# VectorE in place of GpSimd for the low parts of the second MoE's first weights

## The chip, the cores and the metric

The kernel runs on one core of one Trainium2 chip. The metric is the time of one execution in microseconds (us) on the device, the median of several runs. A core has five engines that run side by side, each through its own list of instructions: TensorE (PE; its weight loads are shown as PEld), VectorE (DVE), ScalarE (ACT), GpSimd (POOL) and SyncE (SP), which here issues DMA transfers. An engine takes its instructions strictly in the order in which the program issued them; a wait holds everything behind it on that engine.

## The reference

Three stages in float32, one behind the other:

```python
attn = attention(q_l, k_l, v_l, q_g, k_g, v_g)       # 2 x 544 tokens, 8 heads of 64
x = (attn @ w_a * (attn @ w_b)) @ w_out              # "first MoE": 1088 x 512, d_ff 1536
logits = x @ w_gate                                  # router, 8 experts
expert = argmax(logits); gate = softmax(logits)[expert]
h = relu(x_of_expert @ w1[expert])                   # 512 x 1024 per expert, capacity 288
out = gate * (h @ w2[expert])                        # "second MoE"
```

A token keeps its place in its expert by counting the tokens ahead of it; those over the capacity give zeros. TensorE multiplies in a reduced format (float32r), so each float32 matrix is split in a high part (the value rounded to float32r) and a low part (the rest), and each product is made of three passes: high by high, high by low, low by high.

## The kernel before, in words

`moe1` ends with `down`, the second half of the product with `w_out` (the call with `last`). It goes over nine token tiles: tile 0 (64 tokens, 12 matmuls) and tiles 1 to 8 (128 tokens, 18 matmuls of 128x512 each: six blocks of d_ff by three passes). When a tile's matmuls are through, VectorE adds the result to what the first half left (L797). Behind each matmul `c` (1 to 18) of tile `i` (1 to 8), `steps(i, c, fs)` issues whatever else is due there. `c` is called the step below. All is issued in a fixed order (a manual schedule), so the place of a call in `steps` sets its place in each engine's queue.

Most of it is the router of the tiles before, in three parts whose places are in `ROUTE_AT`:

- `route_t(j)`: four transposes of tile j's rows on TensorE (L905), and the split of the result. For tiles 0 to 4 that is three bf16 parts: ScalarE L887, VectorE L888, ScalarE L889, and later, at step 3 of the tile after, VectorE's `rest` (L892). Tiles 5 to 8 have one copy on ScalarE (L907).
- `route_l(j, k)`: the logits on TensorE (L925 for tiles 0 to 4, L920 for the rest), then some seven small VectorE instructions (L938 to L955) that make the one-hot of the best expert (`roh`, L943) and the count so far (`cnt`, L950, two buffers).
- `route_s(j)`: small matmuls that count places (L963, L966), which need the one-hot and the count, then VectorE makes the slot number (L972, L982, L985; for tiles 6 to 8 also `to`, L978), and GpSimd scatters the tile's rows into their slots in DRAM by an indirect DMA (L988). Tile 5's `route_s` also queues on SP a load of the first 128 slots (`x2c`, L992), which waits for the scatters so far.

In tiles 2 to 5 the logits of tile i-2 and the transposes of tile i-1 come at step 8 (tile 2: steps 6 and 12) and the slots of tile i-2 at step 17 (tile 2: step 12). In tile 6 step 6 has the transposes of tile 5, step 8 the logits of tile 4, step 12 those of tile 5, step 17 the slots of tile 4. In tile 7: step 6 the slots of tile 5 and the transposes of tile 6, step 12 the logits of tile 6. In tile 8: step 6 the transposes of tile 7, step 12 the slots of tile 6 and the logits of tile 7. What is left comes behind the last matmul.

`steps` also prepares the first weights of the second MoE. These come in units of 512x512 (`wt[q]`, four per expert: two of w1, two of w2), each in two halves of 128x1024. For a half, `moe2_first(q, hf)` has ScalarE copy the raw weights to the high part (L566) and GpSimd subtract it from them for the low part (L567). Behind a unit's second half SP is given the load of unit q+4 into the same raw buffer (L572), which therefore waits for L567. The halves of units 0 to 3 are made two per tile at step 2 of tiles 1 to 4, those of unit 4 at steps 9 and 12 of tile 8. The order of work behind that, `moe2`, has semaphores of its own and isn't touched: there VectorE makes most low parts (L1633) and GpSimd one unit per expert (L1778). Its block begins when SP has seen everything ahead of it done.

Of the kernel before, what the change touches and what calls it, by code (L numbers as in the profile page):

```python
# [12 lines left out]
ALU = mybir.AluOpType  # L13
# [11 lines left out]
ROUTE_AT = ((12, 24, 30), (12, 26, 35), (8, 26, 35), (8, 26, 35), (8, 26, 35), (6, 12, 24), (6, 12, 30), (6, 12, 20))  # L25
REST_AT = 21

CONV2_AT, CONV2, CONV2_LAST = 2, (2, 2, 2, 2, 0, 0, 0, 0), (9, 12)

FIRST, FILL = (3, None, 2), (3, 2, 5, 2)  # L30
WARM = (0, 0, 0, 1, 2)
# [7 lines left out]
def attn_moe_moe_kernel(  # L39
# [18 lines left out]
    nc = tc.nc  # L58
# [11 lines left out]
    NTT = (NT + P - 1) // P  # L70
# [466 lines left out]
    NU = 2 * NH  # L537
# [8 lines left out]
    def raw_at(q):  # L546

        return q % NR0 if q < NIN - NXR or not NXR else (q - NIN) % NRAW
# [8 lines left out]
    wt = []  # L557
    raw = []
# [1 line left out]
    xs = []  # L560
    ptx = []

    def moe2_first(q, hf):
        r = raw[raw_at(q)]
        hs = slice(2 * hf, 2 * hf + 2)
        nc.scalar.copy(out=wt[q][:, 0, hs], in_=r[:, hs])  # L566
        nc.gpsimd.tensor_tensor(out=wt[q][:, 1, hs], in0=r[:, hs], in1=wt[q][:, 0, hs], op=ALU.subtract)  # L567
        if hf == 1 and q < NU:
            moe2_load(q + NR0)

    def moe2_load(q, ks=slice(0, 4)):
        nc.sync.dma_start(out=raw[raw_at(q)][:, ks], in_=unit_src(q)[:, ks])  # L572
# [133 lines left out]
    def moe1():  # L706
        with ExitStack() as mx:
# [37 lines left out]
            def steps(i, c, fs):  # L745

                for j in range(max(0, i - 3), min(i, NTT - 1)):
                    at = c + 3 * len(fs) * (i - 1 - j)
                    t, l, r = ROUTE_AT[j]
                    if at == t:  # L750
                        route_t(j)
                    if at == l:
                        for k in range(KD):
                            route_l(j, k)
                    if at == REST_AT and j < N_BF16:
                        rest.pop(j)()
                    if at == r:
                        route_s(j)
                if c == CONV2_AT:
                    o = sum(CONV2[:i - 1])  # L760
                    for k in range(o, o + CONV2[i - 1]):
                        moe2_first(k // 2, k % 2)
                if i == NTT - 1 and c in CONV2_LAST:
                    moe2_first(NU, CONV2_LAST.index(c))

            def down(fs, first, last):
                for x, i in enumerate([*range(1, NTT), 0] if first else range(NTT)):
# [6 lines left out]
                    for f in fs:  # L774
                        if i == 0:
                            parts = ((t[0:2 * n], gtl[f], 0), (t[0:n], gtl[f][:, 0:n], 1))
                        else:
                            parts = tuple((t, g_t[f][:, gi, o:o + n], wi) for gi, wi in passes)
                        for ot, l, wi in parts:
                            nc.tensor.matmul(  # L780
                                out=ot, lhsT=l, rhs=wo[f][:, wi],
                                start=(c == 0), stop=(c == nm - 1), skip_group_check=True)
                            c += 1
                            if last and i > 0:
                                steps(i, c, fs)
# [18 lines left out]
                if last:  # L804
# [22 lines left out]
                    for at in range(3 * len(fs) + 1, 100):  # L827
                        steps(NTT - 1, at, fs)
# [17 lines left out]
                out=x2[:, :, DM + 1:DM + 2], in_=tokid.rearrange("p (t o) -> p t o", o=1))  # L846
# [49 lines left out]
            def route_t(i):  # L896
                n = tok(i)[1]
                x3 = m2.tile([P, KD, 3, P], BF16, tag="rx", name="rx")
                xs = as_f32(x3)
                nh = 2 if i == NTT - 1 else 1  # L900
                for h in range(nh):
                    tx = ps.tile([P, KD // nh, P], F32, tag="rt", name="tx")
                    for j in range(KD // nh):
                        k = h * KD // nh + j
                        nc.tensor.transpose(tx[:, j, 0:n], row(i)[0:n, k * P:(k + 1) * P], ident[0:n, 0:n])  # L905
                    if i >= N_BF16:
                        nc.scalar.copy(out=xs[:, h * KD // nh:(h + 1) * KD // nh, 0:n], in_=tx[:, :, 0:n])  # L907
                if i >= N_BF16:
                    xss[i] = xs
                else:  # L910
                    rest[i] = split3(tx[:, :, 0:n], tx[:, :, 0:n], x3[:, :, :, 0:n])
                    xss[i] = x3
# [85 lines left out]
            for s in range(NGA * HC, len(slots1)):  # L998
                f, c = slots1[s]
                k = s - NGA * HC  # L1000
# [11 lines left out]
                if s == len(slots1) - 1:  # L1012
# [8 lines left out]
                    for q in range(NR0):  # L1021
# [6 lines left out]
                        out=late_x["x"][:, :, DM + 1:DM + 2],  # L1028
                        in_=tokid[:, NTT - 2:NTT].rearrange("p (t o) -> p t o", o=1))
# [821 lines left out]
```

## Time and profile before

| | before |
|---|---|
| median of 3 runs | 499.58 us (498.74 to 504.02) |
| the profiled execution | 499.53 us, span 497.8 us |
| mean granted TensorE clock | 0.976 |
| TensorE busy | 465.2 us (93% of the span) |
| VectorE, ScalarE, GpSimd busy | 299.2, 262.1, 238.4 us |

The span goes from the first to the last instruction in the trace; the time of the execution has some 2 us around it. Busy times of TensorE are modelled, since matmuls are pipelined. The granted clock is a share of 2.4 GHz; 0.5 is the lower of its two levels, 1.2 GHz, and a value between is a mean over a stretch. In a row of the trace the arrow between names goes from inputs to output (`wt<-raw`), `xN` counts instructions that are merged in the row, and what stands in brackets at the end is the idle time of the engine ahead of it and what ended it.

### The profile page before, as it was taken

What the parts mean: (1) busy time and instruction counts of PE and PEld (TensorE: products, weight loads), DVE (VectorE), ACT (ScalarE), POOL (GpSimd) and SP (SyncE); (2) the same over time, 40 slices, a digit from 0 to 9 for tenths busy, and PEclk for the clock granted to TensorE, in tenths of its full rate; (3) what the DMA queues carried; (4) which work ended last, traced back from release to release, by engine and by line L of the source; (5) the groups of instructions that cost most, each with busy time, mean ns of one, the idle gap of its engine ahead of it and who ended that gap; (6) DMA issues with size and microseconds to landing.
All of it is one profiled execution on the core that took longest, in us unless ns stands there. A gap on an engine that the chain in (4) does not pass through costs nothing.

```text
span 497.8 us, 8982 instructions
## 1 busy us (share of the span) xinstructions
PE 465.2 (93%) x3137; PEld 393.6 (79%) x3137; DVE 299.2 (60%) x668; ACT 262.1 (53%) x580; POOL 238.4 (48%) x247
## 2 busy tenths in 40 slices
PE   8899999999999999999999977987979979999993
PEld 6676778899999988899999855776657757768783
DVE  5758799751676456766663269654666537668420
ACT  3878887653444333533333433223677648677330
POOL 2334547542467514555555576146277437366203
PEclk9999999999999999999999989898989989999997
DMA  7794544130688624553504253332698499493001
GB/s 175 177 224 120 144 121 117 50 129 1 205 233 230 191 86 126 165 175 127 170 1 156 98 181 115 118 124 82 163 374 324 134 297 362 134 392 122 9 6 68
DMA packets 76464, 77.53 MB, mean 156 GB/s; under 512 B 39426, under 2 KB 51714, under 8 KB 76392
## 3 DMA queue, kind: packets, MB, share of 16 engines
q1 hardware_dynamic: 74424, 72.32, 47.3%
q0 software_dynamic: 1968, 4.29, 2.3%
q8 instruction: 40, 0.66, 0.6%
q14 instruction: 32, 0.26, 0.2%
HBM read 63.77 MB, written 14.25 MB: 157 GB/s over the span
## 4 chain that ended last, share of the span: by engine, by line
PE 87%; DVE 6%; issue 3%; ACT 1%; DMA 1%; POOL 0%; SPq 0%; POOLq 0%
PE ab L680 29%; PE o L780 13%; PE ph L1385 13%; PE py L1385 11%; PE px L418 4%; PE s L357 3%; PE tp L402 3%; PE pth L1370 2%; DVE rv L940 2%; PE sgm L338 1%; PE og L478 1%; PE ptx L1353 1%; PE tk L263 1%; PE tq L279 1%; DMA kr<-in_k_l_dram 1%
## 5 line engine op out<-in xcount | busy, mean ns | idle before, releaser
L680 PE MATMUL ab<-xT,wab 128*128 128x272 f32 x1152 | 148.6, 290 | 0.0
L680 PEld LDWEIGHTS ab<-xT,wab 128*128 128x128 f32 x1152 | 145.4, 188 | 3.0 <-issue 2.3
L1385 PE MATMUL py<-wt,ht 128*128 128x512 f32 x224 | 57.3, 402 | 0.0
L392 POOL TENSOR_TENSOR pn<-sm,rs 128x384 f32<-128x384 f32 (+1 forms) x32 | 28.6, 895 | 55.8 <-DVE rs L391 36.0
L688 ACT COPY a_sb<-ab 128x272 f32<-128x272 f32 x48 | 18.6, 387 | 68.3 <-PE ab L680 68.3
L695 DVE TENSOR_TENSOR gf<-a_sb,ab 128x272 f32<-128x272 f32 x48 | 20.8, 433 | 51.8 <-PE ab L680 29.7
L780 PE MATMUL o<-wo,g_all 128*128 128x512 f32 x192 | 51.6, 412 | 0.0
L641 POOL TENSOR_TENSOR wab<-cvs,wab 128x512 fp32r<-128x512 f32 x24 | 34.7, 1446 | 27.7 <-ACT wab L640 27.7
L1385 PEld LDWEIGHTS py<-wt,ht 128*128 128x128 f32 x224 | 39.4, 180 | 10.8 <-issue 0.2
L641 POOL TENSOR_TENSOR g_all<-gf,g_all 128x272 fp32r<-128x272 f32 x32 | 27.7, 866 | 39.5 <-ACT g_all L640 39.5
L1633 DVE TENSOR_TENSOR wt<-raw,wt 128x1024 fp32r<-128x1024 f32 x34 | 42.2, 1297 | 4.1 <-ACT wt L1495 4.0
L780 PEld LDWEIGHTS o<-wo,g_all 128*128 128x128 f32 x192 | 37.0, 196 | 8.3
L631 DVE TENSOR_SCALAR cvs<-cvs 128x512 int32<-128x512 int32 x36 | 32.4, 901 | 16.1 <-ACT cvs L626 16.1
L1226 POOL DMA_INDIRECT out_dram<-x2l,ids x14 | 22.6, 1616 | 40.5 <-DVE dummy L1656 22.7
L1495 ACT CAST wt<-raw 128x1024 fp32r<-128x1024 f32 x40 | 39.3, 1055 | 0.1
L634 DVE SCALAR_TENSOR_TENSOR cvs<-raw,cvs 128x512 int32<-128x512 int32 x36 | 38.3, 1063 | 1.2
L1385 PE MATMUL ph<-wt,xs 128*128 128x512 f32 (+1 forms) x128 | 37.4, 411 | 0.5 <-issue 0.5
L380 ACT ACTIVATE sm<-sm,mn 128x192 f32<-128x192 f32 (+1 forms) x64 | 29.4, 462 | 0.2
L357 PE MATMUL s<-kz,qz 128*128 128x192 f32 (+1 forms) x128 | 29.2, 349 | 0.1
L1385 PEld LDWEIGHTS ph<-wt,xs 128*128 128x128 f32 (+1 forms) x128 | 22.9, 183 | 7.7 <-issue 1.3
L632 DVE SCALAR_TENSOR_TENSOR cvs<-raw,cvs 128x512 int32<-128x512 int32 x36 | 26.8, 744 | 1.2
L370 DVE CUSTOM_DVE_ANT_0 sm<-s,mask 128x192 f32<-128x192 f32 (+1 forms) x64 | 21.5, 372 | 9.4 <-PE s L357 8.4
(219 smaller groups left out, 830.8 us busy)
## 6 DMA issues: line engine op xcount, KB each, us to landing
raw<-in_moe_w_dram SPq DMA_DIRECT2D x31, 1024.0 KB, 7.7
slots_dram<-zrow SPq DMA_DIRECT2D x24, 257.0 KB, 6.1
raw<-in_moe_w_a_dram SPq DMA_DIRECT2D x12, 512.0 KB, 4.0
raw<-in_moe_w_b_dram SPq DMA_DIRECT2D x12, 512.0 KB, 3.9
raw<-in_moe_w_out_dram SPq DMA_DIRECT2D x12, 512.0 KB, 4.0
xr<-slots_dram SPq DMA_DIRECT2D x11, 256.0 KB, 2.7
kr<-in_k_l_dram SPq DMA_DIRECT2D x16, 128.0 KB, 2.9
qr<-in_q_l_dram SPq DMA_DIRECT2D x16, 128.0 KB, 2.9
```

Of the source, the lines that this page charges most:

```text
L357: nc.tensor.matmul(out=s[:, h, 0:width(t)], lhsT=qz[i % 2][:, h, t * P:(t + 1) * P], rhs=kz[i % 2][:, t, 0:width(t)], start=True, stop=True)
L380: nc.scalar.activation(out=sm[:, h, 0:w], in_=sm[:, h, 0:w], func=ACTF.Exp, scale=-1.0, bias=mn[:, h:h + 1], accum_out=su[:, h:h + 1])
L392: nc.gpsimd.tensor_tensor(out=pz[:, :, 0:w], in0=sm[:, :, 0:w], in1=rs.rearrange("p (h o) -> p h o", o=1).to_broadcast([P, 2, w]), op=ALU. ...
L631: nc.vector.tensor_scalar(out=s, in0=s, scalar1=3, scalar2=None, op0=ALU.logical_shift_left)
L632: nc.vector.scalar_tensor_tensor(out=s, in0=l, scalar=29, in1=s, op0=ALU.logical_shift_right, op1=ALU.bitwise_or)
L634: nc.vector.scalar_tensor_tensor(out=s, in0=h, scalar=-0x80000000, in1=s, op0=ALU.bitwise_and, op1=ALU.bitwise_or)
L641: nc.gpsimd.tensor_tensor(out=lo, in0=src, in1=hi, op=ALU.subtract)
L680: nc.tensor.matmul(out=t, lhsT=wab[f][:, j, wi, k * P:(k + 1) * P], rhs=xT[:, xi, k, cs], start=(n == 0), stop=(n == 3 * KD - 1))
L780: nc.tensor.matmul(out=ot, lhsT=l, rhs=wo[f][:, wi], start=(c == 0), stop=(c == nm - 1), skip_group_check=True)
L1385: m = tensor.matmul(out=o, lhsT=l, rhs=w(k, wi)[:, cols], start=(k == 0 and i == 0), stop=(k == nk - 1 and i == len(parts) - 1), skip_grou ...
L1495: scalar.copy(out=wt[q % NSLOT][:, 0, 2 * hf:2 * hf + 2], in_=raw[raw_at(q)][:, 2 * hf:2 * hf + 2]).then_inc(sem["sa"], 1)
L1633: m = vector.tensor_tensor(out=wt[q % NSLOT][:, 1, hk], in0=raw[raw_at(q)][:, hk], in1=wt[q % NSLOT][:, 0, hk], op=ALU.subtract)
```

## The change

`moe2_first` is cut in two: `moe2_hi` (ScalarE, as before) and `moe2_lo`, the same subtraction on VectorE, with the load behind the second half as before. The places change too. High parts of units 0 to 3: one half at step 12 of each of tiles 1 to 4, two at step 12 of tiles 5 and 6. The low part of a half comes in the tile after its high part, at step 4, where there are two also at step 14. Unit 4: high parts at steps 6 and 7 of tile 8, low parts at steps 9 and 11. Within a step the router's calls are issued first.

```diff
-CONV2_AT, CONV2, CONV2_LAST = 2, (2, 2, 2, 2, 0, 0, 0, 0), (9, 12)
+SPLIT2, LO_AT, HI_AT = (0, 1, 1, 1, 1, 2, 2, 0), (4, 14), 12
+HI_LAST, LO_LAST = (6, 7), (9, 11)
...
-    def moe2_first(q, hf):
-        r = raw[raw_at(q)]
+    def moe2_hi(q, hf):
         hs = slice(2 * hf, 2 * hf + 2)
-        nc.scalar.copy(out=wt[q][:, 0, hs], in_=r[:, hs])
-        nc.gpsimd.tensor_tensor(out=wt[q][:, 1, hs], in0=r[:, hs], in1=wt[q][:, 0, hs], op=ALU.subtract)
+        nc.scalar.copy(out=wt[q][:, 0, hs], in_=raw[raw_at(q)][:, hs])
+
+    def moe2_lo(q, hf):
+        hs = slice(2 * hf, 2 * hf + 2)
+        nc.vector.tensor_tensor(
+            out=wt[q][:, 1, hs], in0=raw[raw_at(q)][:, hs], in1=wt[q][:, 0, hs], op=ALU.subtract)
         if hf == 1 and q < NU:
             moe2_load(q + NR0)
...
-                if c == CONV2_AT:
-                    o = sum(CONV2[:i - 1])
-                    for k in range(o, o + CONV2[i - 1]):
-                        moe2_first(k // 2, k % 2)
-                if i == NTT - 1 and c in CONV2_LAST:
-                    moe2_first(NU, CONV2_LAST.index(c))
+                if c == HI_AT and i < NTT - 1:
+                    o = sum(SPLIT2[:i])
+                    for k in range(o, o + SPLIT2[i]):
+                        moe2_hi(k // 2, k % 2)
+                if i == NTT - 1 and c in HI_LAST:
+                    moe2_hi(NU, HI_LAST.index(c))
+                if i == NTT - 1 and c in LO_LAST:
+                    moe2_lo(NU, LO_LAST.index(c))
+                if c in LO_AT[:SPLIT2[i - 1]]:
+                    k = sum(SPLIT2[:i - 1]) + LO_AT.index(c)
+                    moe2_lo(k // 2, k % 2)
```

## Rows read from the trace of the kernel before

**Rows 1.** Stretches: us; busy PE, PEld, DVE, ACT, POOL; clock; DMA share; GB/s.

```profile
290.00:300.00 10.00, 7.73 (x42) 6.15 (x42) 6.70 (x16) 3.94 (x7) 7.22 (x4) 0.83 0.54 197
300.00:310.00 10.00, 6.31 (x43) 4.61 (x42) 9.14 (x22) 3.34 (x6) 6.51 (x4) 1.00 0.41 131
310.00:315.00 5.00, 5.00 (x30) 3.76 (x30) 3.32 (x14) 1.23 (x4) 0.99 (x1) 0.66 0.75 262
```

**Rows 2.** The chain that ended last: start us, us, what.

```profile
304.88 4.44 DVE rv L940
...
336.75 2.38 DVE to L978
```

**Rows 3.** Timeline of VectorE, tiles 5 and 6: start, us, engine, line, what.

```profile
313.88 0.18 DVE L938 TENSOR_REDUCE rlo<-lg 128x8 f32<-128x24 f32 x1 [1.45 <-PE lg L925]
...
315.25 0.70 DVE L888 TENSOR_TENSOR tx<-tx,rx 128x512 f32<-128x512 f32 x1
...
316.61 0.17 DVE L972 CUSTOM_DVE_ANT_0 rv<-lg,roh 128x8 f32<-128x8 f32 x1 [0.66 <-PE lg L966]
...
317.79 0.68 DVE L892 TENSOR_TENSOR rx<-tx,rx 128x512 bf16<-128x512 f32 x1
...
319.97 0.23 DVE L940 SCALAR_TENSOR_TENSOR rv<-rlo,rs,desc 128x8 f32<-128x8 f32 x1
...
322.67 0.16 DVE L950 TENSOR_TENSOR cnt<-cnt,roh 128x8 bf16<-128x8 bf16 x1 [0.40 <-PE lg L966]
```

**Rows 4.** Timeline of GpSimd and VectorE, tiles 4 and 8.

```profile
304.58 4.69 POOL L567 TENSOR_TENSOR wt<-raw,wt 128x1024 fp32r<-128x1024 f32 x2
...
332.05 2.38 POOL L567 TENSOR_TENSOR g_all<-raw,g_all 128x1024 fp32r<-128x1024 f32 x1 [2.66 <-ACT g_all L566]
332.20 2.31 DVE L978 TENSOR_SCALAR to<-cols,rs 128x128 f32<-128x128 f32 x1
```

**Rows 5.** TensorE's waits, 284 to 342 us: total us, times, longest.

```profile
PE lg L963 <- DVE roh L943: 5.0, 3, 2.8
PE lg L963 <- DVE cnt L947: 3.1, 1, 3.1
```

**Rows 6.** Low parts by line: count, duration ns min/median/max, first and last start.

```profile
L567 POOL TENSOR_TENSOR wt<-raw,wt x8: 2339/2390/2643, 282.6 to 306.9; 128x1024 fp32r<-128x1024 f32 x8
...
L1633 DVE TENSOR_TENSOR wt<-raw,wt x34: 1206/1219/3426, 353.9 to 460.5; 128x1024 fp32r<-128x1024 f32 x34
```

**Rows 7.** The chain again, tile 5 from its start.

```profile
310.01 3.49 PE o L780 x9
313.50 0.34 PE lg L925 x12
313.84 0.59 PE tx L905 x4
314.44 2.09 PE o L780 x9
```

**Rows 8.** Timeline of TensorE, tile 7 step 6 and behind tile 8.

```profile
324.19 0.10 PEld L963 LDWEIGHTS <-utri 128*128 128x128 bf16 x1 [0.27 <-DVE x L797]
...
335.74 0.18 PE L963 MATMUL lg<-roh,utri 128*128 128x8 bf16 x1 [1.53 <-DVE roh L943]
```

**Rows 9.** Scatters: timeline in the second MoE, and L988 by line.

```profile
421.08 4.63 DVE L1633 TENSOR_TENSOR wt<-raw,wt 128x1024 fp32r<-128x1024 f32 x4
...
421.42 1.76 POOL L1226 DMA_INDIRECT out_dram<-x2l,ids  x1 [1.09 <-DVE ht L1682]
...
L988 POOL DMA_INDIRECT slots_dram<-x,rsi x7: 974/992/1111, 294.0 to 335.2; - x7
```

**Rows 10.** SP: timeline, longest waits; stretch of the last loads.

```profile
332.14 0.94 SPq L572 DMA_DIRECT2D raw<-in_moe_w_dram  x2
...
SPq L1283 <- DVE cnts L880: 2.6, 1, 2.6
...
334.00:336.00 2.00, 0.47 (x5) 0.27 (x5) 1.82 (x11) 0.69 (x3) 1.21 (x2) 1.00 1.02 357
```

## Prediction

> **What bounds the kernel now.** I read the stretches first, then the chain of waits, then what ran beside each long piece of that chain. The last down-projection, with the router of the second MoE threaded through it, runs from about 278 to 342 us. TensorE is the pace-setter there, but two parts of it go badly [rows 1]: between 290 and 310 us TensorE is busy 7.73 + 6.31 of 20 us, and in 290 to 300 and 310 to 315 its granted clock averages 0.83 and 0.66, where 300 to 310 has 1.00.
>
> The chain says what TensorE waits for [rows 2]: VectorE's instructions on a 128x8 or 128x128 tile, which should be tiny: 4.44 us of L940 and 2.38 of L978 are the longest. The same line L940 takes 0.23 us in a quiet tile [rows 3]. The neighbours tell why [rows 4]: GpSimd's pair of low-part subtractions (L567) runs from 304.58 to 309.27, and the L940 that began at 304.88 ends at 309.32; the next one runs from 332.05 to 334.43, and the L978 that began at 332.20 ends at 334.51. So it isn't GpSimd's 2.39 us as such [rows 6] that costs: certain VectorE instructions of the router stand still until GpSimd's instruction is over, and TensorE stands behind them. The list of TensorE's waits gives the bill [rows 5]: 3.1 us for the first count and 5.0 us in three waits for the one-hot (2.8 the longest; 1.53 of them is the one in tile 8 [rows 8]).
>
> **What the change takes away.** All ten L567 leave GpSimd (10 x 2.39 us); its only work left in these tiles is the scatters. The long L940, L943 and L978 should fall to about 0.23 to 0.35 us. Waits gone: 3.1 + (5.0 - 1.53) = 6.6 us; I leave the 1.53 us of tile 8 aside, since low parts stand there after the change too.
>
> The low clock goes with the long waits: the low stretches follow waits of 3.1 and 2.8 us, while those of 0.7 (5.0 - 2.8 - 1.5) and 1.5 us are followed by full clock. The lost clock is 10 x 0.17 + 5 x 0.34 = 3.4 us, which at 1.2 instead of 2.4 GHz is 6.8 us of time at the low level. Nine matmuls and what stands between them took 3.49 us at the low level and 2.09 at the high one [rows 7], so 40% of these 6.8 us is lost: 2.7 us. Gain so far: 9.3 us.
>
> **What the change adds.** VectorE gets ten subtractions of 128x1024. The same operation in the second MoE takes 1.22 us, the median of 34 [rows 6]: 12.2 us of VectorE in all. ScalarE's ten high-part copies only move (to step 12 of tiles 1 to 6 and steps 6 and 7 of tile 8), and nothing on TensorE's path stands behind them in ScalarE's queue until the next tile's step 6 or 8, so they cost nothing while that tile's VectorE is on time.
>
> *Tiles 2 to 5, one low part each at step 4.* It stands in VectorE's queue behind the addition of the tile before and the router's third part (L892), and ahead of the router's logits (L938). A tile's VectorE work in a quiet tile [rows 3]: L972 to L985 and the addition 1.18 (316.61 to 317.79), L892 0.68, L938 to L888 1.37 (313.88 to 315.25), L888 0.70: 3.93 us, with the low part 5.15. TensorE's tile [rows 7]: 18 matmuls at 2.09/9 = 0.23 make 4.18, logits 0.34, transposes 0.59: 5.11. As good as even: VectorE falls back 0.04 us a tile, and the one-hot, ready some 4 us into the tile, is asked for only behind the 17th matmul, at 4.9. I take 0.1 us for tile 2, where it is asked for at step 12, and nothing for tiles 3 to 5. From both sides: nothing, and 1.22 us each, 4.9 us, if it stood wholly in the way.
>
> *Tile 6, two.* The second, at step 14, stands behind L950, which waits for TensorE at step 17 (0.40 us of waiting in the trace of before [rows 3]); so it begins at the end of the tile, and the five small instructions of tile 4's slots and the addition of tile 6 come 1.22 us later. TensorE waits for that addition already (0.27 us, at 324.19 [rows 8]), in front of step 6's transposes in tile 7. So all of it is exposed: 1.2 us. At least 0 (if the low part found room earlier), at most 1.22.
>
> *Tile 7, two.* The second stands ahead of tile 7's addition again, but there the logits come earlier in the tile, and the addition ends some 1.9 us into tile 8 where its transposes want it at about 1.4: 0.45 us. Between 0 and 1.22.
>
> *Tile 8, two.* The first high part can't come before ScalarE has copied step 6's transposes, as before, when GpSimd began the low part at 332.05 [rows 4]. Two on VectorE last from there to 334.5, just when GpSimd let L978 go before. Behind them L972 and L978 (0.2 + 0.35 us) are still to come, so the one-hot of tile 7 is 0.6 us later and TensorE's wait about 2.1 instead of 1.53 us. Then the second L978 isn't held for 2.38 us any more [rows 2], which brings 0.3 us back, limited by the logits it ran beside. Net 0.35. Between a gain of 1.5 and a loss of 1.3 us.
>
> *Transfers.* Weights of units 4 to 7 are now loaded when VectorE has made the low part. The last (tile 7, step 14) stands on SP's queue behind the load of the first rows from the slots, which waits for tile 5's scatter; so it goes out with the two halves that left at 332.14 [rows 10], and one more MB lands in front of them. At the 357 GB/s of 334 to 336 us that is 2.9 us. SP's last wait at the entry of the second MoE was 2.6 us for the counts [rows 10], so the transfers had landed by then; with the tail 0.35 later the cover is 2.95. I take nothing; without the cover it costs its 2.9 us. Units 5 and 6 have more than a tile to spare.
>
> *Scatters.* GpSimd writes the scatters' descriptors while VectorE subtracts: in the second MoE such a scatter takes 1.76 us where these take 0.99, while the four subtractions beside it stay at 4.63 / 4 = 1.16 [rows 9]. So a scatter may lose 0.8 us, on an engine with nothing else to do, and VectorE nothing. The Trainium skill, SBUF — State Buffer, section Who interferes with whom, says that a VectorE instruction with two SBUF inputs contends with a GpSimd instruction that reads SBUF, and that the second to issue stands fully still; by that a low part, which has two SBUF inputs, could be held by a scatter. The rows here show the scatter slowed, not the low part; no run here shows the opposite.
>
> Sum: 9.3 - 0.1 - 1.2 - 0.45 - 0.35 = 7.2 us. The profiled execution took 499.53 us (span 497.8), beside a median of 499.58: 499.53 - 7.2 = 492.3.
>
> **The rivals.**
> 1. *VectorE's queue becomes the bound in every tile.* 5.15 against 5.11 us says it could; for it: VectorE is busy 9.14 of 10 us in 300 to 310 already [rows 1], against it: most of that is the hold itself. If tiles 2 to 5 and 7 lose 0.7 us each beyond the above, 3.5 us: 495.8.
> 2. *Slower: each low part delays the router's chain whole.* Place: VectorE's queue, at each of the ten. Price: 12.2 us, and the waits stay long enough that the clock still falls, so only 6.6 is gained: 499.5 - 6.6 + 12.2 = 505.1. It decides from an excess of 0.66 us per low part on. Against it: the low part stands at step 4, and the one-hot is wanted at step 17.
> 3. *The holds aren't GpSimd's doing* and stay: nothing gained, 2.1 lost: 501.6. Against it: the two ends agree to 0.1 us.
> 4. *The late loads hold the entry*: up to 2.9 us: 495.2; likelier 1 us, 493.3. For it: the cover is as large as the transfer.
> 5. *Scatters hold the low parts*: seven by 0.99, 6.9 us: 499.2. Against it [rows 9]. The page named above would have it so.
>
> **How the numbers follow.** The forecast 0.67 (490 to 494.4), rival 4 0.08, rival 1 0.12, rival 2 0.06, rival 3 0.04, rival 5 0.03. About 1% (5 us) is what a measurement here can tell from no change. The forecast and rival 4 lie below 494.6: faster 0.75. Rivals 1, 3 and 5 lie within 1%: 0.19. Rival 2 lies above: 0.06. The range: at the low end the whole 9.3 plus the 1.5 us of tile 8, 488.7, rounded to 489; at the high end rival 1, with some room, 496.5; what lies outside is rivals 2, 3 and 5, 0.13, and a few hundredths below.
>
> **What would show it.** Right: no L940, L943 or L978 above 0.5 us; low parts of about 1.2 us on VectorE; TensorE's wait at 3.1 and 2.8 us gone and the clock at 1.0 from 278 us to the end of tile 8; a wait of 1 to 1.5 us in front of tile 7's transposes and of about 2 us behind tile 8. The second MoE takes as long as before from its first matmul on. Wrong: TensorE waits for the one-hot or for L892 in tiles 3 to 5 (rival 1 or 2); long L940 beside an idle GpSimd (rival 3); SP waits for the weights at the entry (rival 4). If tile 8's longer wait sent the clock down, some 1 to 1.5 us would come on top.

## The result

| | before | after |
|---|---|---|
| median | 499.3 us (496.31 to 504.02, 8 runs) | 493.0 us (490.38 to 495.88, 8 runs) |
| ratio | | 0.9884, 95% interval 0.985 to 0.9918 |
| the profiled execution | 499.53 us, span 497.8 | 491.78 us, span 490.1 |
| GpSimd busy | 238.4 us | 216.1 us |

The forecast was 492.3 us in 489.0 to 496.5, faster. It came true, but not for all of its reasons: one term was left out, others made up for most of it, and that the two nearly cancelled is luck. Runs over 1.5% above the fastest of their kernel are left out of all ratios; the profiled execution of the last kernel in part 5 (494.66 us) is one of them, so its trace is read for waits and for what came behind what, and its span is left alone.

The stretches first: us; busy PE, PEld, DVE, ACT, POOL; clock; DMA share; GB/s. They answer to [rows 1].

```profile
290.00:300.00 10.00, 10.00 (x71) 7.89 (x70) 8.68 (x25) 5.01 (x11) 2.10 (x2) 1.00 0.46 147
300.00:310.00 10.00, 10.00 (x72) 7.64 (x72) 9.24 (x32) 5.99 (x12) 1.97 (x2) 1.00 0.50 153
...
326.00:340.00 14.00, 10.04 (x54) 9.26 (x55) 5.12 (x31) 3.98 (x11) 4.58 (x8) 0.76 0.55 192
```

TensorE has no idle time left in 290 to 310 us (14.04 of 20 us busy before) and its clock is full. But in the last line, behind tile 8, the clock averages 0.76. In the trace of before 326 to 340 had 1.00.

The timeline of VectorE and TensorE in tile 4 of the changed kernel, which answers to [rows 3] and [rows 4] (line numbers are ten higher: L950 was L940, L898 was L888):

```profile
297.89 1.22 DVE L571 TENSOR_TENSOR wt<-raw,wt 128x1024 fp32r<-128x1024 f32 x1
...
299.02 0.17 DVE L948 TENSOR_REDUCE rlo<-lg 128x8 f32<-128x24 f32 x1
...
299.43 0.23 DVE L950 SCALAR_TENSOR_TENSOR rv<-rlo,rs,desc 128x8 f32<-128x8 f32 x1
...
299.88 0.23 DVE L953 TENSOR_SCALAR roh<-rv,rs 128x8 bf16<-128x8 f32 x1
...
300.98 0.18 PE L973 MATMUL lg<-roh,utri 128*128 128x8 bf16 x1
```

L950 takes 0.23 us where the same line in the same tile (then L940) took 4.44, and the low part ahead of it takes 1.22. The one-hot (L953) is ready at 300.11; TensorE asks for it (L973) at 300.98, 0.9 us later.

The waits of TensorE from 278 to 340 us (total us, times, longest), which answer to [rows 5]:

```profile
PE lg L973 <- DVE roh L953: 1.8, 1, 1.8
...
PE tx L915 <- DVE x L807: 0.9, 1, 0.9
```

Where 8.1 us of waiting for the count and the one-hot stood in two rows, 1.8 are left, and the new wait for the addition has come (0.9). The two places in the timeline, as in [rows 8], with the second low part of tile 6, the first of tile 7 and the scatter that runs beside it:

```profile
312.59 1.22 DVE L571 TENSOR_TENSOR wt<-raw,wt 128x1024 fp32r<-128x1024 f32 x1
...
314.90 1.22 DVE L571 TENSOR_TENSOR wt<-raw,wt 128x1024 fp32r<-128x1024 f32 x1
315.04 0.66 PE L915 MATMUL tx<-ident,x 128*128 128x128 f32 x4 [0.88 <-DVE x L807]
...
315.14 1.83 POOL L998 DMA_INDIRECT slots_dram<-x,rsi  x1 [6.38 <-DVE x L807]
...
327.20 0.18 PE L973 MATMUL lg<-roh,utri 128*128 128x8 bf16 x1 [1.81 <-DVE roh L953]
```

From the start of L973 behind tile 8 to the router's last matmul it was 335.74 to 342.10 us before, 6.4 us; now it is 327.20 to 336.05, 8.9 us. The last rows of that part, at the low clock:

```profile
331.53 1.63 PE L746 MATMUL ptx<-ident,x2c 128*128 128x128 f32 x6
```

Six such matmuls took 0.92 us before. So the account of the two traces is: 8.5 us earlier at that L973 (335.74 to 327.20), 2.5 given back behind it, 6.0 at the first matmul of the second MoE (344.68 to 338.69). The medians differ by 6.3. The further 1.7 us by which the spans differ lie in the second MoE, and I don't count them: from its first matmul to the end, the traces of this study and the two above lie between 150 and 158 us, and I see no order in them that follows what was changed. What makes them differ stays open.

### The profile page after: what moved, and what is told of

Same layout as the page of the kernel before. It is cut to its first block, busy times and chain, and to the rows that moved or that the text cites. A ratio compares the mean times of both kernels' runs of the same rounds, so it can differ in the third digit from the quotient of the medians.

```text
span 490.1 us, 8980 instructions
## 1 busy us (share of the span) xinstructions
PE 464.2 (95%) x3137; PEld 393.5 (80%) x3137; DVE 299.9 (61%) x678; ACT 261.8 (53%) x580; POOL 216.1 (44%) x237
## 4 chain that ended last, share of the span: by engine, by line
PE 90%; DVE 4%; issue 3%; ACT 1%; DMA 1%; DVEq 0%; POOL 0%; SPq 0%; POOLq 0%
PE ab L685 30%; PE ph L1395 14%; PE o L790 14%; PE py L1395 11%; PE px L420 4%; PE s L359 4%; PE tp L404 3%; PE pth L1380 2%; PE sgm L340 1%; PE og L480 1%; PE ptx L746 1%; PE ptx L1363 1%; PE tk L265 1%; PE tx L915 1%; PE tq L281 1%
## 5 line engine op out<-in xcount | busy, mean ns | idle before, releaser
L790 PE MATMUL o<-wo,g_all 128*128 128x512 f32 x192 | 49.4, 399 | 0.0
L1643 DVE TENSOR_TENSOR wt<-raw,wt 128x1024 fp32r<-128x1024 f32 x34 | 43.6, 1335 | 4.4 <-ACT wt L1505 4.2
L790 PEld LDWEIGHTS o<-wo,g_all 128*128 128x128 f32 x192 | 35.4, 188 | 7.8
L636 DVE TENSOR_SCALAR cvs<-cvs 128x512 int32<-128x512 int32 x36 | 31.2, 868 | 16.1 <-ACT cvs L631 16.1
```

Source lines behind the costliest of these rows:

```text
L636: nc.vector.tensor_scalar(out=s, in0=s, scalar1=3, scalar2=None, op0=ALU.logical_shift_left)
L790: nc.tensor.matmul(out=ot, lhsT=l, rhs=wo[f][:, wi], start=(c == 0), stop=(c == nm - 1), skip_group_check=True)
L1643: m = vector.tensor_tensor(out=wt[q % NSLOT][:, 1, hk], in0=raw[raw_at(q)][:, hk], in1=wt[q % NSLOT][:, 0, hk], op=ALU.subtract)
```

## Experiments

**1. Is it the engine or the places?** The change does two things. One kernel has the new places with GpSimd:

```diff
     def moe2_lo(q, hf):
-        nc.vector.tensor_tensor(
+        nc.gpsimd.tensor_tensor(
```

> The changed kernel with the low parts back on GpSimd, at the new places. Theory (the engine and the place both count; a hold costs only where it outlasts the slack of a tile): L940 in tiles 2 to 5 is held again, up to 2.4 us, but by one low part and not two, so the one-hot comes at most 1 us later than in the changed kernel, where it has about 0.9 us to spare; TensorE's waits in tiles 2 to 5 stay under 0.7 us each, L978 in tile 8 is held again as before: 494 to 496 us, most of the gain kept. Rival (the engine alone): any low part on GpSimd beside the router stops TensorE as before; waits of 2 to 3 us and low clock return in tiles 2 to 5, 497 to 500 us. Rival (the place alone): as fast as the changed kernel or faster, 491 to 493.

Measured: 498.22 us, ratio 1.0003 (0.9971 to 1.0035): none of the gain. The chain of waits (start us, us, what):

```profile
293.66 1.49 DVE rv L950
...
299.19 2.14 DVE rv L950
...
305.37 2.11 DVE rv L950
...
311.94 3.99 DVE rv L950
...
323.35 3.17 DVE roh L953
```

There is a hold (a small VectorE instruction that stands until GpSimd's is over) in every tile from 2 on, where before had them in 2, 3, 4 and 8, and in tile 6 the pair holds for 4 us. My theory for this kernel was wrong: I had GpSimd begin a low part as soon as ScalarE had copied its high part. In fact its scatter of an older tile stands ahead, which waits for VectorE's addition, so the low part begins later, just ahead of L950 (298.88 for the L950 of 299.19). TensorE's waits for the one-hot in tiles 4 and 5 are only 0.5 us each, as I had expected, but VectorE's lateness goes from tile to tile: from one L950 to the next it is 6.2 us there (299.19 to 305.37), where the changed kernel has 5.1.

The other has VectorE at the old places:

```diff
     def moe2_first(q, hf):
...
-        nc.gpsimd.tensor_tensor(out=wt[q][:, 1, hs], in0=r[:, hs], ...
+        nc.vector.tensor_tensor(out=wt[q][:, 1, hs], in0=r[:, hs], ...
```

> The kernel before with VectorE making the low parts where GpSimd did, both halves of a unit directly behind their high parts at step 2. Theory: the low parts wait in VectorE's queue for two high parts that are copied in the same tile (2 x 1.05 us) and stand ahead of L892, which TensorE wants at step 8; L892 then ends about 4.5 us into a tile instead of 1.7, so TensorE waits some 2.5 us in each of tiles 2 to 4 and the clock may fall: 498 to 503, no gain or a loss. Rival (the engine alone counts): the hold is gone, so nearly the whole gain is there: 491 to 494.

Measured: 502.3 us, ratio 1.0107 (1.0031 to 1.0183), slower. TensorE's waits:

```profile
PE lg L925 <- DVE rx L892: 7.1, 3, 2.7
```

Three waits of up to 2.7 us for L892, as expected: the pair of low parts stands ahead of it. No L940, L943 or L978 is held in this trace. So neither half of the change alone brings anything. VectorE takes away the hold, and only the new places keep VectorE's own queue off TensorE's path.

**2. What is held?** GpSimd stays as it was, but the router's small tiles move to PSUM:

```diff
-                v = m2.tile([P, E], F32, tag="rv", name="rv")
+                v = lg[:, 1] if i < N_BF16 else m2.tile([P, E], F32, tag="rv", name="rv")
...
-                    lo = m2.tile([P, E], F32, tag="rlo", name="rlo")
+                    lo = lg[:, 3]
```

> The kernel before, low parts on GpSimd at their old places; for tiles 0 to 4 the summed logits and the weighted comparison are kept in PSUM instead of SBUF, so that L940, L942 and L943 read at most one operand from SBUF (L940 still reads the constants there). Theory (GpSimd holds those VectorE instructions that read two operands from SBUF, or that copy from SBUF to SBUF): L940 and L943 take 0.2 to 0.3 us beside a GpSimd subtraction, and the hold moves on to L950, which adds two operands from SBUF; the total is as before, 497 to 500. Rival (VectorE's small instructions stand still for another reason, whatever they read): L940 or L943 still take 2 to 4 us beside L567.

Measured in a single run: 494.68 us, span 492.9. GpSimd and VectorE in tile 4 (timeline):

```profile
299.67 4.69 POOL L567 TENSOR_TENSOR wt<-raw,wt 128x1024 fp32r<-128x1024 f32 x2
...
299.79 0.23 DVE L940 SCALAR_TENSOR_TENSOR lg<-lg,rs,desc 128x8 f32<-128x8 f32 x1
300.26 0.23 DVE L943 TENSOR_SCALAR roh<-lg,rs 128x8 bf16<-128x8 f32 x1
300.52 3.87 DVE L950 TENSOR_TENSOR cnt<-cnt,roh 128x8 bf16<-128x8 bf16 x1
```

L940 and L943 run at their quiet 0.23 us beside GpSimd, with the same sizes; what differs is where their operands lie (for L940 the output too). The hold has moved on to L950, the next that reads two tiles in SBUF, and ends at 304.39 with GpSimd's pair (304.36). The Trainium skill, SBUF — State Buffer, section Who interferes with whom, says just this of VectorE instructions with two SBUF inputs; these rows agree. An instruction need not read two tiles to stand, though: the L978 of before (2.38 us) reads one tile and two columns of scalars, and the first tile's hold here is a copy, all of them from SBUF to SBUF. The time came out under my 497 to 500: that copy's hold is 1.17 us, and tile 3's shrank to 0.72, as each now begins later beside the same GpSimd work. In this trace the first matmul of the second MoE comes at 339.39 us, 5.3 sooner than before: with GpSimd at its old work and its old places, nearly the 6.0 of the change. It is a single run, so it doesn't show that the time would follow.

**3. How near was VectorE to being the bound?** The changed kernel with four more low parts:

```diff
-        nc.vector.tensor_tensor(
...
+        for _ in range(2 if q < 2 else 1):
+            nc.vector.tensor_tensor(
...
```

> The changed kernel with each low part of units 0 and 1 made twice (four more subtractions of 1.22 us, one each in tiles 2 to 5). Theory (VectorE and TensorE are as good as even there, 5.15 against 5.11 us a tile): VectorE sets the pace, each of tiles 2 to 5 is 1.0 to 1.3 us longer, 497 to 498 us in all. Rival (VectorE has slack, so that rival 1 and 2 of the prediction were never near): 0 to 2 us longer, 493 to 495.

Measured: 497.62 us, ratio to before 0.9987 (0.9953 to 1.0021), so 1.0% more than the changed kernel's 0.9884, 5 us for 4.9 us of work. From one-hot to one-hot a tile takes 6.1 us (302.61 to 308.75 in the chain; the line is L954 in this kernel), where the changed kernel has 5.12 (299.88 to 305.00), and VectorE is the chain:

```profile
299.43 1.14 DVE wt L572
300.60 1.23 DVE wt L572
...
302.61 0.24 DVE roh L954
```

The tiles up to the transposes of tile 5 cost 3.3 us (307.90 to 311.17). The rest of the 5 us isn't theirs. The wait at the entry of the second MoE (TensorE's, ahead of its first matmul) is 4.2 us in this trace instead of 2.6, which was the first sign of what part 5 is about; but behind tile 8 the clock stayed up, which gave 2.9 back, so that first matmul comes only 2.0 us later than in the changed kernel (338.69 to 340.73). The other 3 us lie in the second MoE, and no run shows why. So the estimate "as good as even" holds, as the tiles show it: one more low part per tile makes VectorE the bound.

**4. The waits that the change left.** The changed kernel again beside three others, all on one chip. "Second at 9" has the first change of this diff, "unit 4 later" the second, "both" has both:

```diff
-SPLIT2, LO_AT, HI_AT = (0, 1, 1, 1, 1, 2, 2, 0), (4, 14), 12
+SPLIT2, LO_AT, HI_AT = (0, 1, 1, 1, 1, 2, 2, 0), (4, 9), 12
-HI_LAST, LO_LAST = (6, 7), (9, 11)
+HI_LAST, LO_LAST = (6, 7), (13, 21)
```

> The changed kernel itself, on the same chip as the next three, as their measure. Theory: about 1.2% faster than before, the wait behind tile 8 about 1.8 us; where the clock falls behind it, the stretch from there to the end of the router is some 2.5 us longer than where it doesn't.

> The changed kernel with the two low parts of unit 4 at step 13 of tile 8 and behind the slots of tile 7, instead of steps 9 and 11. Theory (they stand ahead of the router's one-hot in VectorE's queue and make the 1.8 us wait behind tile 8, and with it the fall of the clock): the wait for the one-hot there goes to under 0.3 us, some 1.2 us of waiting for the addition may take its place, granted clock 1.0 to the end of the router: 2 to 4 us faster than the changed kernel. Rival (the wait only moves to the addition of tile 8 and the clock falls as it did): within 1 us of the changed kernel.

> The changed kernel with the second low part of tiles 6 and 7 at step 9 instead of 14, ahead of the router's logits of step 12. Theory (at step 14 it is pushed behind an instruction that waits for TensorE, and delays the addition by a whole low part): the waits for the addition in front of the transposes of tiles 7 and 8, 0.9 and 0.5 us, shrink to 0.3 or less: 0.8 to 1.4 us faster than the changed kernel. Rival (VectorE has no room there either): the wait turns up at the slots of tile 4 or the logits of tile 5, no gain.

> Both moves of the two kernels before. Theory: their gains add, 3 to 5 us faster than the changed kernel, some 2% faster than the kernel before; rival: the tail's gain alone, since what tiles 6 and 7 give up is waited for behind tile 8 on a copy of ScalarE or on the load of the first rows.

| kernel | ratio to before (interval) | router's last matmul, us | wait for the entry, us | first matmul of the second MoE, us |
|---|---|---|---|---|
| changed | 0.989 (0.9846 to 0.9935) | 336.1 | 2.6 | 338.66 |
| unit 4 later | 0.9858 (0.9814 to 0.9903) | 331.3 | 5.2 | 336.54 |
| second at 9 | 0.9853 (0.9809 to 0.9896) | 332.1 | 3.6 | 335.71 |
| both | 0.9854 (0.9798 to 0.991) | 329.9 | 4.9 | 334.75 |

By time none of the three is told apart from the changed kernel: the intervals overlap, and the 2 to 5 us that I had expected of "unit 4 later" and "both" aren't shown. The traces say what happened. With unit 4 later the wait for the one-hot behind tile 8 is gone and the clock stays up: the six matmuls that took 1.63 us take 0.91, and the router ends 4.7 us sooner. With the second low part at step 9 the waits of 0.9 and 0.5 us are gone, as expected. But the wait at the entry grows by 1.0 to 2.6 us and eats a quarter to over a half of what the router gains. Its row in the kernel with unit 4 later (TensorE's waits), and SP's:

```profile
PE py L1433 <- issue: 5.2, 1, 5.2
```

```profile
SPq L1293 <- DMA slots_dram<-x,rsi: 8.5, 1, 8.5
```

SP stands at the block's entry for 8.5 us until a scatter has landed. That is now the wait that ends last; before, the one for the counts did (2.6 us in [rows 10]).

One thing stays open here. The wait behind tile 8 is 1.81 us in both traces of the changed kernel, and the clock fell within 2 us. It is 1.85 in the kernel with the second low part at 9 and 1.81 in that of part 3, and there the clock stayed up through the router. Nor does a longer wait always bring it down: in the kernel with VectorE at the old places, TensorE waited 2.45 us for L892, and the stretches around that wait and behind it have full clock:

```profile
289.13 0.48 PE L925 MATMUL lg<-wg,rx 128*64 128x24 bf16 x10 [2.45 <-DVE rx L892]
...
288.00:290.00 2.00, 0.87 (x12) 0.80 (x13) 1.39 (x4) 0.00 (x0) 0.00 (x0) 1.00 0.53 203
290.00:292.00 2.00, 2.00 (x13) 1.44 (x12) 1.41 (x12) 0.39 (x2) 0.00 (x0) 1.00 0.73 276
```

So the wait alone doesn't settle the clock. What does, these runs don't show. The stretches of 2 us behind the wait, the changed kernel and then the one with the second at 9 (us; busy PE, PEld, DVE, ACT, POOL; clock; DMA; GB/s):

```profile
326.00:328.00 2.00, 0.80 (x7) 0.80 (x8) 1.82 (x11) 0.36 (x2) 0.49 (x1) 0.94 1.02 348
328.00:330.00 2.00, 2.00 (x12) 2.00 (x11) 0.52 (x4) 0.74 (x2) 1.15 (x3) 0.50 1.05 372
330.00:332.00 2.00, 2.00 (x11) 2.00 (x11) 0.25 (x2) 0.00 (x0) 0.00 (x0) 0.50 1.03 339
```

```profile
326.00:328.00 2.00, 1.88 (x18) 1.81 (x18) 1.41 (x9) 0.64 (x3) 1.69 (x3) 1.00 1.01 372
328.00:330.00 2.00, 2.00 (x21) 2.00 (x20) 0.93 (x6) 0.41 (x3) 0.00 (x1) 1.00 1.01 336
330.00:332.00 2.00, 2.00 (x17) 1.67 (x15) 1.31 (x11) 0.20 (x1) 0.63 (x2) 1.00 0.45 180
```

**5. Which transfer holds the entry?** The kernel with both moves, once without unit 7's load:

```diff
-        if hf == 1 and q < NU:
+        if hf == 1 and q < NU - 1:
             moe2_load(q + NR0)
```

> The kernel with both moves (second low part at step 9, unit 4 at step 13 and behind tile 7's slots), with the load of unit 7's weights left out, so that the second expert uses wrong weights in one unit: a measure of what that transfer costs. In the kernel with both moves the router ended at 329.8 us and the second MoE's first matmul came 4.9 us later, because SP waited at the entry until 332 us for tile 6's scatter to land, which shared the DMA engines with 2.3 MB of loads. Theory (that late load, queued behind the load of the first rows, holds the scatter and so the entry): the wait at the entry returns to 2.6 us and the second MoE begins some 2.3 us earlier, 487 to 490 us. Rival (the scatter is late by itself): the wait stays at 4 us or more.

Measured: ratio 0.9788 (0.9747 to 0.9829); the wait at the entry is 2.6 us again and the second MoE's first matmul comes at 332.59, 2.2 us sooner. SP's waits:

```profile
SPq L1293 <- DMA slots_dram<-x,rsi: 5.7, 1, 5.7
SPq L1293 <- DVE cnts L890: 0.6, 1, 0.6
```

The counts end last again. So it is that one MB: SP gives it out behind the load of the first rows, and tile 6's scatter, issued some 3 us later, lands behind it.

And once with the load sooner, nothing left out:

```diff
-SPLIT2, LO_AT, HI_AT = (0, 1, 1, 1, 1, 2, 2, 0), (4, 14), 12
-HI_LAST, LO_LAST = (6, 7), (9, 11)
+SPLIT2, LO_AT, HI_AT = (0, 1, 1, 1, 1, 2, 2, 0), (4, 5), 12
+HI_LAST, LO_LAST = (6, 7), (13, 21)
```

> As with both moves, but the second low part of tiles 6 and 7 at step 5, right behind the first; nothing left out. The load of unit 7 then goes out ahead of the load of the first rows and some 3 us sooner. Theory: the wait at the entry shrinks from 4.9 to about 3 us, the router ends within 0.7 us of the kernel with both moves: 1 to 2 us faster than it, 2% faster than the kernel before. Rival (the low part at step 5 delays tile 5's slots and so its scatter and the load of the first rows by 1.2 us, and TensorE waits for these rows): no faster, a wait at the first rows of 1 us or more.

Measured: 488.41 us, ratio 0.9787 (0.9757 to 0.9817). That is clear of before and of the changed kernel (0.985 to 0.9918): the best kernel of the study. Against the kernel with both moves the intervals overlap. Its trace has the wait at the entry at 2.6 us, and the rival's wait too, half as long as the rival wanted it:

```profile
PE py L1433 <- issue: 2.6, 1, 2.6
...
PE ptx L746 <- DMA x2c<-slots_dram: 0.5, 1, 0.5
```

The load isn't free at its new place either. It now goes out ahead of tile 5's scatter, and from that scatter's start to the load of the first rows, which waits for it, this trace has 4.5 us (320.20 to 324.74), where the kernel with both moves has 3.2 (318.18 to 321.39). And behind that wait of 0.5 us and one of the same length for tile 8's addition the clock fell in this execution too, as these six matmuls show:

```profile
328.75 1.63 PE L746 MATMUL ptx<-ident,x2c 128*128 128x128 f32 x6
```

## Why the prediction was right, and where it wasn't

- *The holds are GpSimd's doing.* Right, and shown twice: they are gone with VectorE at the new places and at the old ones, back with GpSimd at the new places (part 1), and they follow the operands in SBUF (part 2).
- *The low clock goes with the long waits.* Right for what the change does from 290 to 315 us: 1.00 throughout. As a rule it is too simple: it fell behind 1.81 us here and stayed up behind 1.85 and 2.45 elsewhere (part 4).
- *What is taken away, 9.3 us.* By the start of L973 behind tile 8 the changed kernel is 8.5 us ahead. The sum had 9.3 - 0.1 - 1.2 - 0.45 - 0.6 = 6.95 there, so it was short by 1.6 us. Two thirds of that lie in what is taken away: tile 6 begins 10.3 us sooner, where 9.3 - 0.1 = 9.2 stood. Both parts of it were a little small: TensorE also waited 0.22 us for L892 in tile 4, each wait cost 0.1 to 0.2 us more than its row says, and the low clock cost 3.0 us rather than 2.7. The other third lies between there and that L973, where 1.7 us are lost and 2.25 stood (the next three points). The first matmuls of tile 6, before and now:

```profile
316.75 1.55 PE L780 MATMUL o<-wo,g_all 128*128 128x512 f32 x6
...
306.49 1.57 PE L790 MATMUL o<-wo,g_all 128*128 128x512 f32 x6
```

- *Tiles 2 to 5 cost nothing.* Right: 5.12 us a tile, where 5.11 and 5.15 were the estimates, and part 3 shows that the margin was as thin as they said.
- *Tiles 6 and 7, 1.2 and 0.45 us.* The waits came at the places named, for the reasons named. From the first matmuls of tile 7 to those behind its transposes it is now 1.0 us longer, and 0.3 in tile 8. One reading was wrong: the 0.27 us in [rows 8] was no wait of TensorE for the addition. It stands in a row of weight loads, and the same line has it where the addition isn't due, and has it still:

```profile
331.63 0.10 PEld L963 LDWEIGHTS <-utri 128*128 128x128 bf16 x1 [0.28 <-issue]
...
313.95 0.10 PEld L973 LDWEIGHTS <-utri 128*128 128x128 bf16 x1 [0.27 <-DVE rs L982]
```

- *Tile 8: a wait of about 2.1 us.* 1.81, so the one-hot's delay cost 0.3 us where 0.6 stood.
- *The tail, net 0.35.* Wrong, and the largest miss. (By its own terms, 0.6 and 0.3, it is 0.3.) "If tile 8's longer wait sent the clock down, some 1 to 1.5 us would come on top" stood under what would make the prediction wrong, not in the sum. In both traces of the changed kernel it did come down, and from L973 to the end of the router it took 8.9 us instead of 6.4 with the hold and 5.95 in the kernel with the second low part at step 9, where the clock stayed up: 2.9 us, twice what I had put. It should have been a term with a chance of its own.
- *The loads cost nothing.* Right for the changed kernel, by a thin margin: SP's wait for the counts, the last to end, is 1.3 us there, where it was 2.6. I had it that the loads' own landing was at risk. Part 4 shows the risk in another shape: the scatter behind them.
- *The scatters lose 0.8 us, the low parts nothing.* Right where a scatter starts beside a running low part: 1.83 us for the one at 315.14, and the low part stays at 1.22. The other six take 0.98 to 1.11. Three of them start some 0.35 us ahead of a low part, and neither is longer for it, so rival 5, a scatter that holds a low part, had its chance three times in this trace and didn't come. The first of the three:

```profile
297.55 0.99 POOL L998 DMA_INDIRECT slots_dram<-x,rsi  x1 [5.58 <-DVE x L807]
...
297.89 1.22 DVE L571 TENSOR_TENSOR wt<-raw,wt 128x1024 fp32r<-128x1024 f32 x1
```

So the forecast of 7.2 us, against 6.3 by the medians and 6.0 to the first matmul of the second MoE, is right in its mechanism, but it lay this near by luck: two errors went most of the way to cancel, 1.6 us too little gained up to tile 8's end, and 2.8 too little lost behind it (2.5 lost, where 0.25 of gain stood).

## What to carry to other kernels

A long duration of a tiny VectorE instruction is a wait in disguise: look what GpSimd runs at that moment and where both ends lie. Moving work to a faster engine frees nobody unless its new place in that engine's queue stands behind what the critical engine will ask for next; here the engine alone and the places alone brought nothing or a loss. And a load that is issued later, though hidden itself, can hold a small transfer behind it that isn't.

## What the runs showed of the hardware

- An instruction of 128x8 that adds two SBUF tiles stands 3.87 us beside GpSimd's subtraction, while one of the same size with an input in PSUM takes 0.23 (part 2).
- A scatter on GpSimd takes 1.83 us when it starts beside a running VectorE subtraction of two SBUF operands, and 0.98 without one or when it starts 0.35 us ahead of it; the subtraction takes 1.22 each time.
- After waits of equal length (1.81 to 1.85 us) TensorE's granted clock fell to 1.2 GHz in two traces of one kernel and stayed at 2.4 in those of two others; behind one of 2.45 us it stayed at 2.4 as well.
